# Pooled attention and a bilinear layer on one Trainium2 core: the PSUM tile of the scores, split into five tiles of one bank for the last stage

## The chip, the cores and the metric

The kernel runs on one core of one Trainium2 chip. The metric is the time of one execution on the device in microseconds (us). The engines are named as the profile names them: PE multiplies matrices (PEld is its load of weights), DVE is the vector engine, ACT the scalar engine, POOL the third one for element-wise work, and SP issues the transfers. PE writes its products into PSUM, from where DVE and ACT read them.

## The reference

An attention with pairwise averaged queries feeds a bilinear layer, all in single precision:

```
q_pool = q.reshape(B, H, S // 2, 2, D).mean(axis=3)        # B, H, S, D = 4, 8, 1152, 64
scores = (q_pool @ k.T) / sqrt(D)
attn   = softmax(scores)                                    # with 1e-9 in the divisor
x      = (attn @ v)  as 2304 tokens x 512
out    = ((x @ w_a) * (x @ w_b)) @ w_out                    # 512 -> 1536 -> 512
```

## The kernel before, in words

**Precision.** Most operands are held as a pair of 16-bit numbers, a high and a low part, and a product is the sum of three: high by high, high by low, low by high. So one logical product is a run of several matmuls into one place in PSUM.

**Stages.** The attention goes over 16 pairs of heads in blocks of 128 query rows: scores on PE (`qk`, lines 789 and 791) into `sps`, the running maximum on DVE (`sm_max`, line 821), the exponential and the division on ACT and DVE (lines 828 to 845), a transposing transfer, and the product with v (line 942). The bilinear layer works on nine tiles of 256 tokens. Tiles 0 to 6 go one after the other, between the heads of the attention, each in 12 column blocks: `moe_mm` (line 1023) makes the two products, ACT and DVE multiply them (`moe_a`, `moe_g`), ACT and POOL split the result into its two parts (`moe_gh`, line 1066; `moe_gl`, line 1069), and `moe_o` (line 1089) adds its six matmuls to the output.

**The last stage.** The last two tiles, 7 and 8, are worked jointly, from about 706 us to 831 us of the trace. For each column block f, PE makes seven products (`joint`, line 1263), each six matmuls of 128x256, from sums of weights and sums of tokens. ACT copies the first (`c_copy`, line 1266), DVE adds the others up in seven additions (`c_add`, line 1269) and multiplies the two results (`c_g`, line 1273). Then come `moe_gh`, `moe_gl` and two `moe_o`, one for each tile, of six matmuls of 128x512. In between DVE and POOL prepare the sums of weights for the blocks ahead (`t_sum` line 1203, `t_mix` line 1209, `t_hi` line 1213, `t_lo` line 1217; `bal_w` line 1200).

**Where the products land.** `sps` is one tile of 2560 columns, five banks of 512. In the attention it holds the scores of one block. In the last stage it holds the seven products, which go round four of the banks by `place(f, n)` and use the second half of each, and in the fifth bank one half of the output of tile 7. The other output halves are in `xps` (tile 7) and in `ab0` and `ab1` (tile 8).

```
ab = [PT(f"ab{j}", [128, 2, TOK]) for j in range(2)]
xps = PT("xps", [128, 512])
sps = PT("sps", [128, 2560])
def place(f, n):
    return (len(TURN) * f + TURN.index(n)) % 4
def wide(f, n):
    return sps[:, 512 * place(f, n) + TOK:512 * place(f, n) + 2 * TOK]
```

**What sets the order.** The kernel is described as 3009 tasks, each with the names that it reads and writes (`P0` to `P3` for the four places). A table written out by hand, `ORDERS`, gives the order of the tasks on each of PE, DVE, ACT, POOL and SP. Small products that fill gaps on PE (`idle`, line 651, and `warm`, line 655) are tasks of this table too. The waits themselves are not in the table: the tile framework derives them from which instruction touches which tile.

Of the kernel before, what the change touches and what calls it, by code (L numbers as in the profile page):

```python
# [7 lines left out]
F32 = mybir.dt.float32  # L8
# [32 lines left out]
TOK = 256  # L41
# [56 lines left out]
    ),  # L98
    (
# [240 lines left out]
def kernel(  # L340
# [66 lines left out]
    def PT(name, shape):  # L407
        return ps.tile(shape, F32, name=name)

    sps = PT("sps", [128, 2560])  # L410
    ab = [PT(f"ab{j}", [128, 2, TOK]) for j in range(2)]
    xps = PT("xps", [128, 512])
    sums = xps[:, 510:512]
# [660 lines left out]
    def out_bank(t, u):  # L1074
        if t not in sums_in:
            return acc[u]
        at = sums_in[t][u]
# [447 lines left out]
```

## Time and profile before

| what | value |
|---|---|
| time, median of 3 runs | 837.97 us (835.53 to 839.47) |
| the profiled execution: its time | 840.58 us |
| the profiled execution: its span, first to last instruction | 838.8 us |
| PE busy | 772.4 us, 92% |
| DVE busy | 710.1 us, 85% |
| ACT busy | 574.7 us, 69% |
| POOL busy | 209.6 us, 25% |
| mean granted clock of PE | 0.985 |

The profiled execution is 2.6 us above the median and 1.8 us longer than its own span. Busy PE is modelled: a matmul counts as busy until its result has left, so a run of matmuls that stands alone counts as longer than the same run between others. The idle time before an instruction is put down to the instruction that released it. The rows on which the prediction rests stand further down.

### The profile page before, as it was taken

The page shows a single profiled execution, that of the slowest core. Times are in us where ns is not written, and L with a number is a line of the kernel's source. Part 1 is how long each engine was busy: PE and PEld are TensorE (multiplying, and loading weights), DVE is VectorE, ACT ScalarE, POOL GpSimd, SP SyncE. Part 2 cuts the span into 40 slices and gives each one's busy share as a digit, 9 for nine tenths or more (in the row PEclk, how much of TensorE's full clock was granted, in tenths as well). Part 3 has the DMA queues.
Part 4 walks back from the last instruction along what each step waited for, and adds up shares of the span by engine and source line. Part 5 has one row for each costly group of instructions (what it writes and reads, how often), then busy time and mean ns, then how long its engine had stood idle before and what let it go on. Part 6 is the DMA issues. An engine that isn't in the chain of part 4 may idle for free. (4 is left out here: it accounts for less than half of the span.)

```text
span 838.8 us, 21778 instructions
## 1 busy us (share of the span) xinstructions
PE 772.4 (92%) x8976; PEld 574.6 (69%) x8976; DVE 710.1 (85%) x1411; ACT 574.7 (69%) x960; POOL 209.6 (25%) x269
## 2 busy tenths in 40 slices
PE   9899899999999999999999989999999998677775
PEld 7686687756777667875886578758866884454553
DVE  5988899999889999888899998999899868666572
ACT  6999898898777877677778877777788643212221
POOL 1445141123102321104011401051013251233411
PEclk9999699999999999999999999999999999999998
DMA  8647699999999998778999987998799610000001
GB/s 326 209 131 249 159 259 260 222 206 209 213 185 197 186 198 202 156 170 159 184 198 214 165 214 154 165 186 163 154 196 170 139 31 0 26 1 1 1 0 52
DMA packets 316436, 132.36 MB, mean 158 GB/s; under 512 B 300848, under 2 KB 302896, under 8 KB 316336
## 3 DMA queue, kind: packets, MB, share of 16 engines
q1 hardware_dynamic: 316336, 130.96, 74.5%
q8 instruction: 70, 1.15, 0.6%
q14 instruction: 30, 0.25, 0.1%
HBM read 50.72 MB, written 4.72 MB: 66 GB/s over the span
## 5 line engine op out<-in xcount | busy, mean ns | idle before, releaser
L1023 PE MATMUL ab<-xt,wab 128*128 128x256 f16 x2016 | 229.6, 273 | 0.9 <-DVE st L832 0.5
L1023 PEld LDWEIGHTS <-wab 128*128 128x128 f16 x2016 | 194.7, 99 | 27.1 <-issue 1.8
L828 ACT ACTIVATE s<-s,st 128x1152 f32<-128x1152 f32 x144 | 179.7, 1248 | 34.7 <-DVE s L821 34.5
L845 DVE SCALAR_TENSOR_TENSOR p<-s,st,p 128x1152 f16<-128x1152 f32 x128 | 183.9, 1443 | 11.3 <-ACT p L841 10.1
L841 ACT ACTIVATE p<-s,st 128x1152 f16<-128x1152 f32 x128 | 158.9, 1248 | 39.3 <-issue 12.1
L1069 POOL TENSOR_TENSOR gl<-g,gh 128x256 f16<-128x256 f32 x96 | 75.4, 792 | 332.4 <-ACT gh L1066 254.9
L1089 PE MATMUL ab<-wo,gh 128*128 128x512 f16 x384 | 114.9, 380 | 0.2
L942 PE MATMUL xps<-pt,vs 128*64 128x128 f16 (+1 forms) x3888 | 108.5, 215 | 1.7 <-DVE ksc L477 0.7
L942 PEld LDWEIGHTS <-vs 128*64 128x64 f16 x3888 | 100.7, 110 | 12.9 <-issue 10.2
L821 DVE TENSOR_SCALAR_CACHE_REDUCE s<-sps 128x1152 f32<-128x1152 f32 x72 | 96.4, 1349 | 10.3 <-PE sps L789 8.1
L821 DVE TENSOR_SCALAR_CACHE_REDUCE s<-sps,ksc 128x1152 f32<-128x1152 f32 x72 | 100.7, 1410 | 2.7 <-PE sps L791 1.9
L789 PE MATMUL sps<-k,q 64*128 64x512 f32 (+2 forms) x480 | 89.8, 506 | 3.9 <-DVE s L821 3.6
L1066 ACT ACTIVATE gh<-g 128x256 f16<-128x256 f32 x108 | 42.9, 407 | 61.3 <-DVE g L1273 24.7
L789 PEld LDWEIGHTS sps<-k,q 64*128 64x128 f32 (+1 forms) x480 | 59.4, 178 | 34.6 <-issue 20.7
L1089 PE MATMUL ab<-wo,gl 128*128 128x512 f16 x192 | 72.8, 379 | 1.9 <-POOL gl L1069 1.1
L1089 PEld LDWEIGHTS <-gh 128*128 128x128 f16 x432 | 39.7, 99 | 42.4 <-issue 5.1
L791 PE MATMUL sps<-k,q 64*128 64x512 f16 (+2 forms) x720 | 65.6, 324 | 3.3 <-DVE s L821 3.1
L791 PEld LDWEIGHTS <-q 64*128 64x128 f16 (+1 forms) x720 | 40.2, 96 | 30.6 <-issue 10.1
L1058 ACT ACTIVATE g<-ab 128x256 f32<-128x256 f32 x84 | 30.8, 373 | 32.9 <-PE ab L1023 32.6
L1061 DVE SCALAR_TENSOR_TENSOR g<-ab,cc,g 128x256 f32<-128x256 f32 x84 | 39.6, 478 | 16.2 <-ACT g L1058 15.8
L1203 POOL TENSOR_TENSOR s<-wab 128x512 f32<-128x512 f16 x24 | 30.3, 1272 | 65.9 <-DVE s L1209 19.1
L1266 ACT ACTIVATE q<-sps 128x256 f32<-128x256 f32 x12 | 4.6, 383 | 58.5 <-PE sps L1263 43.6
(195 smaller groups left out, 1030.6 us busy)
## 6 DMA issues: line engine op xcount, KB each, us to landing
k<-in_k_dram SPq DMA_DIRECT2D x18, 576.0 KB, 5.2
vraw<-in_v_dram SPq DMA_DIRECT2D x17, 576.0 KB, 4.4
raw<-in_w_ab_dram SPq DMA_DIRECT2D x18, 512.0 KB, 4.4
qraw<-in_q_dram SPq DMA_DIRECT2D x12, 576.0 KB, 4.7
raw<-in_w_out_dram SPq DMA_DIRECT2D x8, 512.0 KB, 4.8
out_dram<-o SPq DMA_DIRECT2D x16, 256.0 KB, 2.6
xt<-in_w_ab_dram SPq DMA_DIRECT2D x6, 512.0 KB, 4.6
pt<-p SPq DMA_TRANSPOSE x128, 5.4
```

The costliest lines, as they stand in the source:

```text
L789: return nc.tensor.matmul(out, q, k, start=True, stop=True)
L791: return nc.tensor.matmul(out, q[:, hq], k[:, hk], start=(hq, hk) == (0, 0), stop=(hq, hk) == (1, 0))
L821: nc.vector.tensor_scalar(out=s_t[sbuf(i)], in0=sps[:, at:at + S], scalar1=-1.0 / 16.0 if u is None else ksc[:, u, 4:5], scalar2=None, op0 ...
L828: nc.scalar.activation(out=s, in_=s, func=AF.Exp, scale=-1.0, bias=t[:, 0:1], accum_out=t[:, 1:2])
L841: nc.scalar.activation(out=p_t[pbuf(i)][:, 0], in_=s_t[sbuf(i)], func=AF.Copy, scale=st_t[i % NST][:, 3:4])
L845: nc.vector.scalar_tensor_tensor(out=p[:, 1], in0=s, scalar=st_t[i % NST][:, 3:4], in1=p[:, 0], op0=ALU.mult, op1=ALU.subtract)
L942: nc.tensor.matmul(xps[half(e), at:at + w], vs[:, c, e, hv], pt[t][:, hp, c, c0:c0 + w], start=(c == 0 and n == 0), stop=(c == NCH - 1 and ...
L1023: nc.tensor.matmul(dst if t < 8 else dst.rearrange("p (b n) -> p b n", b=B), wab[:, f, 1 - m, a, c], moe_x(t, b, c), start=(n == 0), stop= ...
L1061: nc.vector.scalar_tensor_tensor(out=g_t[:, f], in0=ab[j][:, 0], scalar=cc[:, t, f:f + 1], in1=g_t[:, f], op0=ALU.mult, op1=ALU.mult)
L1066: nc.scalar.activation(out=gh_t[j], in_=g_t[:, f], func=AF.Copy)
L1069: (nc.vector if dve else nc.gpsimd).tensor_tensor(out=gl_t[j], in0=g_t[:, f], in1=gh_t[j], op=ALU.subtract)
L1089: nc.tensor.matmul(out_bank(t, u), g[:, us], wo[:, f, a], start=(first and n == 0), stop=(last and n == 2))
```

## The change

After the last scores have been read, the tile `sps` is given back and its five banks are taken again as five tiles of one bank each (`bank(0)` to `bank(4)`). The seven products go to the first half of `bank(0)` to `bank(3)`, in the same turn, and the output half of tile 7 to `bank(4)`. To be able to give the tile back, `sps` has a pool of its own, which is made after `ab` and `xps`. All five lists of `ORDERS` are new. They hold the same 3009 tasks: none is added, none is left out, and what each computes and waits for by name is the same. Lines after the change are ten further down in this part of the file (1263 becomes 1273, 1269 becomes 1279).

```diff
 ORDERS = (
     (
-        2, 72, 56, 66, 12, 48, 61, 3, 4, 5, 91, 92, 6, 7, 52, 65, 8, 49, 18, 105, 117, 103, 109, 107, 9, 74, 64, 111,
...
+        60, 54, 70, 2, 3, 4, 5, 28, 6, 91, 92, 7, 23, 8, 22, 77, 10, 74, 105, 103, 117, 109, 107, 11, 172, 111, 9,
...
-    sps = PT("sps", [128, 2560])
     ab = [PT(f"ab{j}", [128, 2, TOK]) for j in range(2)]
     xps = PT("xps", [128, 512])
+    scores_pool = tc.tile_pool(name="scores", bufs=1, space=bass.MemoryType.PSUM)
+    sps = scores_pool.__enter__().tile([128, 2560], F32, name="sps")
+    bank_t = []
+
+    def bank(j):
+
+        if not bank_t:
+            scores_pool.__exit__(None, None, None)
+            pool = ctx.enter_context(tc.tile_pool(name="banks", bufs=1, space=bass.MemoryType.PSUM))
+            bank_t.extend(pool.tile([128, 512], F32, name=f"bank{n}") for n in range(5))
+        return bank_t[j]
...
         at = sums_in[t][u]
-        return xps if at is None else sps[:, at:at + 512]
+        return xps if at is None else bank(at // 512)
...
     def wide(f, n):
-        return sps[:, 512 * place(f, n) + TOK:512 * place(f, n) + 2 * TOK]
+        return bank(place(f, n))[:, 0:TOK]
```

PE in the last stage, column block f = 4, before: the products in their order, each shown by the row with which it begins (its five further matmuls and the loads of weights are left out). `sps_122` is the tile, `p1_87` holds the sums of weights of this block, `raw2`, `raw3`, `xr` and `xt1` the tokens, and a wait names the engine on whose count of finished instructions the row waits.

```order
L1263 MATMUL sps_122<-raw3_100,p1_87 128x256 [waits DVE_49]
...
L1263 MATMUL sps_122<-raw2_99,p1_87 128x256
...
L1263 MATMUL sps_122<-xt1_64,wab_61 128x256 [waits Activation_49]
...
L1263 MATMUL sps_122<-raw2_99,p1_87 128x256 [waits DVE_49]
...
L1263 MATMUL sps_122<-xr_65,p1_87 128x256 [waits DVE_49]
...
L1263 MATMUL sps_122<-raw3_100,wab_61 128x256
...
L1089 MATMUL sps_122<-wo_62,gh0_93 128x512 [waits DVE_49]
```

The same block after the change:

```order
L1273 MATMUL bank3_10157<-raw2_99,p1_87 128x256 [waits DVE_49]
...
L1273 MATMUL bank1_10155<-raw2_99,p1_87 128x256
...
L1273 MATMUL bank0_10154<-xt1_64,wab_61 128x256 [waits Activation_49]
...
L1273 MATMUL bank2_10156<-raw3_100,p1_87 128x256 [waits DVE_49]
...
L1099 MATMUL bank4_10158<-wo_62,gh0_93 128x512
...
L1273 MATMUL bank2_10156<-raw3_100,wab_61 128x256 [waits DVE_49]
...
L1273 MATMUL bank1_10155<-xr_65,p1_87 128x256
```

Each product now names the bank that it writes; the product with `xr` and the output product into `bank4` begin without a wait for DVE, and two output products (the one shown, and one into `ab0` and `ab1`) stand between the products of the block.

DVE in the last stage, the additions of the same block, before:

```order
L1269 SCALAR_TENSOR_TENSOR q0_78<-sps_122,q0_78 128x256 [waits PE_49,Activation_49]
L1269 SCALAR_TENSOR_TENSOR x32_66<-sps_122,q0_78 128x256 [waits DVE_49,PE_49]
L1200 TENSOR_SCALAR wab_61<-wab_61,bal_121 128x1024
L1269 SCALAR_TENSOR_TENSOR q1_79<-sps_122,q0_78 128x256 [waits PE_49]
L1269 SCALAR_TENSOR_TENSOR q1_79<-sps_122,x32_66 128x256 [waits DVE_49]
...
L1269 SCALAR_TENSOR_TENSOR q0_78<-sps_122,q0_78 128x256 [waits PE_49]
L1269 SCALAR_TENSOR_TENSOR q1_79<-sps_122,q1_79 128x256
L1269 SCALAR_TENSOR_TENSOR x32_66<-sps_122,x32_66 128x256
```

And after:

```order
L1279 SCALAR_TENSOR_TENSOR x32_66<-bank2_10156,q0_78 128x256 [waits DVE_49,PE_49]
L1279 SCALAR_TENSOR_TENSOR q1_79<-bank3_10157,q0_78 128x256
L1279 SCALAR_TENSOR_TENSOR q1_79<-bank2_10156,q1_79 128x256 [waits DVE_49,PE_49]
L1279 SCALAR_TENSOR_TENSOR q1_79<-bank3_10157,x32_66 128x256
L1279 SCALAR_TENSOR_TENSOR q0_78<-bank0_10154,q0_78 128x256
L1279 SCALAR_TENSOR_TENSOR x32_66<-bank1_10155,x32_66 128x256 [waits DVE_49,PE_49]
```

The preparation that stood among the additions (line 1200, and four subtractions where the dots are) has gone to other places; the additions of this block follow one another in another order.

PE at the very start of the program, before (`xps<-one` are the filling products, `sps` the first scores, `ab<-g,s` transposes):

```order
L651 MATMUL xps<-one 128x256
L655 MATMUL xps<-one 128x96 x6
L651 MATMUL xps<-one 128x256 x3
L789 MATMUL sps<-k_74,q_78 128x512
```

And after:

```order
L665 MATMUL xps<-one 128x96 x3
L661 MATMUL xps<-one 128x256 x4
L665 MATMUL xps<-one 128x96
L661 MATMUL xps<-one 128x256
L799 MATMUL sps<-k_74,q_78 128x512
```

The filling products are the same 78 in all, dealt out anew over the whole program; some that stood in the attention now stand in front of the last stage.

## Rows read from the trace of the kernel before

**Rows 1.** The page, section 4: the chain that ended last, by engine and line.

```profile
PE 26%; DVE 8%; issue 2%; ACT 1%; DMA 0%; SPq 0%; DVEq 0%; ACTq 0%
PE ab L1023 7%; PE sps L1263 6%; PE ab L1089 5%; PE xps L942 3%; PE sps L791 2%; DVE q L1269 2%; DVE x L1269 1%; DVE p L845 1%; PE sps L1089 1%; ACT q L1266 0%; PE xps L1089 0%; DVE s L821 0%; DVE g L1273 0%; DVE pt L1217 0%; DVE s L1209 0%
```

**Rows 2.** Busy time of each engine in five stretches; the first line names the columns.

```profile
core 0: us, PE busy (x) PEld busy (x) DVE busy (x) ACT busy (x) POOL busy (x), PEclk, DMA share, GB/s
0.00:105.00 105.00, 94.10 (x730) 74.30 (x730) 87.05 (x194) 89.47 (x171) 40.46 (x79) 0.90 0.66 215
105.00:650.00 545.00, 528.92 (x7018) 395.98 (x7014) 500.16 (x936) 431.06 (x667) 114.97 (x135) 1.00 0.99 192
650.00:706.00 56.00, 54.47 (x599) 42.01 (x594) 44.18 (x95) 28.05 (x58) 19.56 (x17) 1.00 0.31 64
706.00:831.00 125.00, 94.90 (x645) 62.33 (x643) 77.93 (x187) 25.41 (x67) 34.59 (x38) 1.00 0.01 5
831.00:839.00 8.00, 0.00 (x0) 0.00 (x0) 0.75 (x1) 0.69 (x1) 0.00 (x0) 0.67 0.48 132
```

**Rows 3.** Waits of PE from 706 to 831 us: total, times, longest.

```profile
PE sps L1263 <- DVE q L1269: 15.4, 23, 0.9
PE sps L1263 <- DVE x L1269: 7.5, 11, 1.5
PE sps L1263 <- ACT q L1266: 3.2, 7, 0.5
PE sps L1089 <- DVE q L1269: 2.2, 3, 0.8
PE sps L1089 <- DVE x L1269: 1.0, 2, 0.5
PE sps L1089 <- ACT q L1266: 0.5, 1, 0.5
```

**Rows 4.** Waits of DVE in the same stretch.

```profile
DVE q L1269 <- PE sps L1263: 25.4, 27, 3.4
DVE x L1269 <- PE sps L1263: 9.3, 10, 1.2
DVE q L1269 <- PE sps L1089: 5.8, 5, 1.6
```

**Rows 5.** Timeline within block 4: start, duration, instruction, idle time before it and releaser.

```profile
747.37 0.81 PE L1263 MATMUL sps<-xt,wab 128*128 128x256 f16 x6 [0.47 <-ACT q L1266]
748.29 0.42 DVE L1269 SCALAR_TENSOR_TENSOR q<-sps,q 128x256 f32<-128x256 f32 x1 [0.57 <-PE sps L1263]
748.77 0.82 PE L1263 MATMUL sps<-raw,p 128*128 128x256 f16 x6 [0.58 <-DVE q L1269]
749.62 0.43 DVE L1269 SCALAR_TENSOR_TENSOR x<-sps,q 128x256 f32<-128x256 f32 x1 [0.91 <-PE sps L1263]
...
750.10 0.82 PE L1263 MATMUL sps<-xr,p 128*128 128x256 f16 x6 [0.52 <-DVE x L1269]
750.75 0.82 PE L1263 MATMUL sps<-raw,wab 128*128 128x256 f16 x6
751.61 0.43 DVE L1269 SCALAR_TENSOR_TENSOR q<-sps,q 128x256 f32<-128x256 f32 x1 [1.17 <-PE sps L1263]
...
752.42 0.59 PE L1089 MATMUL sps<-wo,gh 128*128 128x512 f16 x2 [0.85 <-DVE q L1269]
```

**Rows 6.** Stretch 706 to 831 us: line 1263 alone, then line 1089 (PE, PEld, clock).

```profile
706.00:831.00 125.00, 61.89 (x489) 47.17 (x487) 1.00 0.01 5
...
706.00:831.00 125.00, 36.95 (x156) 15.16 (x156) 1.00 0.01 5
```

**Rows 7.** Timeline of PE: products without a wait between them.

```profile
767.18 2.12 PE L1263 MATMUL sps<-raw,p 128*128 128x256 f16 x18 [0.40 <-ACT q L1266]
...
828.12 0.59 PE L1089 MATMUL sps<-wo,gh 128*128 128x512 f16 x2
...
829.42 0.59 PE L1089 MATMUL ab<-wo,gh 128*128 128x512 f16 x2
```

**Rows 8.** Busy time by engine, columns as in the second group, in a stretch of the attention.

```profile
88.00:104.00 16.00, 12.67 (x97) 10.20 (x98) 12.84 (x31) 12.47 (x24) 1.49 (x4) 0.57 0.65 148
```

316 rows, old and new, of the table ORDERS are left out of this document.

## The prediction, on record before the change was run

> **What bounds the kernel now.** I read the busy time by stretch first, then the waits of the stretch that stands out, then its timeline. The chain that ended last shows PE ahead of all others, but it names `sps` of line 1263 and the additions of line 1269 side by side [rows 1], and it shows a quarter of the span only, so the stretches decide. From 105 to 650 us PE is busy 528.9 of 545 us, that is 97%, with DVE at 92%; from 650 to 706 us again 97% [rows 2]. There PE is the bound. From 706 to 831 us, the joint work on the last two tiles, PE is busy 94.9 of 125 us, DVE 77.9, POOL 34.6, ACT 25.4, the transfers next to nothing, and the clock stands at full speed [rows 2]. No engine is full there: something makes them take turns.
>
> The waits say what. PE's waits in this stretch add up to 15.4 + 7.5 + 3.2 + 2.2 + 1.0 + 0.5 = 29.8 us, and every one of them ends with a read of `sps` by DVE or ACT [rows 3]. That is all of PE's idle time (125 - 94.9 = 30.1). At the same time DVE waits 25.4 + 9.3 + 5.8 = 40.5 us for PE to write `sps` [rows 4]. Each waits for the other. The timeline shows the pattern in block 4: a product of six matmuls takes 0.82 us, an addition starts 0.03 to 0.1 us after it, and the next product starts 0.05 us after that addition has ended, and so on in turn [rows 5]. Four products and the step to the output take from 747.37 to 752.42, 5.05 us [rows 5].
>
> The products go round four banks, so a product should have to wait only for the reader of the product four places back. In the built kernel it does not: of the products into `sps` in this stage that wait for a count of DVE or ACT instructions, I followed the count to the instruction that it names, and in 54 of 58 cases it reads another bank than the product writes, as a rule the bank of the product just made. The framework keeps the books for the whole tile. The additions suffer the same way: many wait for a later product than the one that they read.
>
> **The change part by part.** *The split.* With five tiles the books are kept by bank. The same count on the changed kernel gives 56 cases out of 56 in which the read waited for is of the bank that is written, and none of another. So the taking of turns goes, and what is late next is either PE itself or an honest wait: product n+4 for the reader of product n.
>
> What PE needs at least: 489 matmuls of 128x256 and 156 of 128x512 lie in the stretch [rows 6]. Back to back, 18 of the first kind take 2.12 us, which with 0.27 us for the last is 1.85 / 17 = 0.109 us each; six of the second kind go from 828.12 to 829.42, 0.217 us each [rows 7]. 489 x 0.109 + 156 x 0.217 = 53.3 + 33.8 = 87.1 us. The busy time of 94.9 us is larger since each lone product also counts the 0.16 us in which its result leaves. So 125 - 87.1 = 37.9 us is the most that the split can give: 29.8 of waits and 8.1 of such ends.
>
> What stays idle: PE needs 87.1 / 12 = 7.3 us for a block, DVE 77.9 / 12 = 6.5 us, so DVE has 0.8 us of room in each block, not much. The low end is the 3% at which PE idles from 105 to 650 us, with DVE nearly as loaded there [rows 2]: 87.1 / 0.97 is 2.7 us of idle time. The high end is half of today's 37.9, 19 us: the chain through one block stays (copy on ACT, seven additions, two multiplications), the five small buffers of the additions are shared by all blocks, and the copy of the next block must wait for the multiplication that reads its buffer. Today's row prices such a step at some 0.5 us, in the wait for ACT [rows 5], and the new order of DVE puts preparation of later blocks in that place in ten of eleven blocks. PE has up to four products (2.6 us) and one or two output products (1.3 us each) in hand while DVE does such a piece. I take 7 us, nearer to the row of 3% since the loads are like those there, with some more for the first block, where PE waits for the sums of tokens, and the last, where nothing is left to overlap. The stretch then lasts 87.1 + 7 = 94 us, and the gain is 125 - 94 = 31 us, between 19 and 35.
>
> *Giving the tile back.* The first write to a new tile waits until all scores have been read. The table already put the products behind that point, the waiting instruction is on PE, and the last scores are read before the tile 6 products, of which 54 us of busy PE lie in between [rows 2]. This costs nothing here. The end behind the last matmul, 8 us of output steps and stores [rows 2], is the same work in the same order: nothing.
>
> *First half of the bank in place of the second, and other banks for `ab`, `xps` and `sps`.* Same shapes, same banks apart; the rows of 128x256 writes are all 0.27 us, whichever of the four places. I set nothing.
>
> *The new order outside the last stage.* All five lists are dealt anew, DMA issues on SP included, with the same tasks. From 105 to 650 us PE has 16 us of idle time in all [rows 2]; a better order can win a part of it, a worse one can add about as much. In the first 105 us PE stands at a mean clock of 0.90, and between 88 and 104 us at 0.57 with 12.7 us busy [rows 8]: at full speed that work would need some 5 us less, and a second stretch like it would cost as much. I set nothing for all this, with 8 us to either side, as there is no row that speaks for a sign.
>
> A rule of the notes speaks against the split. Rows first: the kernel before goes round four banks, and PE still waits 29.8 us for the reads [rows 3]. The Trainium skill (Perfetto Trace Analysis, section "Optimizing Tensor Performance", on matmuls) says that independent groups of matmuls should rotate through different banks so that the evacuation of one overlaps the next group's matmuls. By that rule the overlap would be there already and the split would give nothing; the trace does not agree, as rotating the banks alone did not bring the overlap.
>
> **Sum.** 840.6 us is the profiled execution. Less 31 gives 809.6 us. It stood 2.6 us above the median of the runs, so against the median I forecast 838.0 - 31 = **807 us**.
>
> **The rivals.** *The chain of one block takes over.* If the copy, the additions and the weights prepared just in time keep half of the idle time, the stretch takes 87.1 + 19 = 106 us and the kernel 838.0 - 19 = 819 us. For it: DVE needs nine tenths of PE's time per block. Against it: the additions that today wait 40.5 us for PE [rows 4] are late because PE is, and PE is late because they are; both ends of that loop go.
>
> *The split does not do what it says.* The readers of a bank are late in fact, not by the books; then the waits [rows 3] stay under new names, and the time is 838 us, give or take the new order. Against it: in the timeline PE starts 0.05 us after a read of another bank [rows 5], three free places notwithstanding.
>
> *Slower than before: the clock of the first stage.* The filling products stand elsewhere now, and some have left the attention for the place in front of the last stage. PE ran at 0.57 from 88 to 104 us when its work came in small pieces [rows 8]. If the new places leave it at the lower of its two levels, 1.2 of 2.4 GHz, for a longer time, every microsecond of work there takes two. This eats the gain of 31 us once 31 us of work at full speed runs at half, a stretch of 62 us; for all of the first 105 us, with 94.1 x 0.90 = 85 us of work at full speed, it would be 170 - 94 = 76 us more, 883 us. Against it: nine fillers in place of ten stand before the first scores, as many as before in all, and DVE and ACT set much of the pace there (87 and 89 of 105 us), so PE has some room.
>
> **How the numbers follow.** Forecast, 807 us: 0.82. Chain of a block, 819: 0.11. No effect, 838: 0.03. Slower by the clock or by a bad new order: 0.04. For the range I put the bounds of the parts together: the stretch from 4 us better (2.7 in place of 7 us idle) to 12 us worse, the rest 8 us to either side, not both at their ends: 807 - 9 = 798 and 807 + 14 = 821, which takes in the rival of the chain. Chances: faster by over 0.5% (4.2 us, about what a measurement of this kernel can tell from no change) 0.82 + 0.11 + 0.01 = 0.94, within 0.5% 0.03 (no effect), slower 0.03; of the last case's 0.04 I leave 0.01 to an order that eats only a part of the gain.
>
> **What would show it.** In the profile after: the joint stage lasts some 94 us in place of 125; PE busy there is 93% or more; waits of PE for DVE and ACT on the banks fall from 29.8 us to under 7 in all; waits of DVE for PE fall from 40 us to around 15; most products stand in runs of several without a gap. The stretch from 105 us to the joint stage keeps its length within 8 us. The forecast is wrong if PE's waits in the joint stage stay above 15 us, or if the granted clock in the first 105 us is well below 0.90.

## The result, and the profile after

The changed kernel takes 804.62 us (median of 4 runs, 803.08 to 807.17), the kernel before 838.6 us beside it. The ratio is 0.960, with a 95% interval of 0.957 to 0.964. The profiled execution takes 803.89 us, 36.7 us less than the 840.58 us of before. In a second, later series the changed kernel took 810.76 us (6 runs, 803.1 to 813.83), at a ratio of 0.967 (0.963 to 0.970). The ten runs together have a median of 807.3 us. What differs between the two series is told with the last experiments.

Where the 36.7 us come from is read with one mark in either kernel: the first product of the joint work, which adds `xt` times `wab` to one of the four places. The rows give count, shortest, median and longest matmul in ns, and the first and the last start. First before, then after:

```profile
L1263 PE MATMUL sps<-xt,wab x144: 269/272/283, 689.7 to 821.2; 128*128 128x256 f16 x144
```

```profile
L1273 PE MATMUL bank<-xt,wab x144: 272/273/273, 688.8 to 786.5; 128*128 128x256 f16 x144
```

Before, the joint work lasts from 689.75 to the last matmul at 830.88, 141.1 us. After, it lasts from 688.84 to 793.96, 105.1 us. That is 36.0 us less. All that comes ahead of it gained 0.9 us in this execution, and the output behind it takes 8 us as before. So the whole gain lies in the joint work.

The busy time by stretch shows the same. The columns are those of [rows 2]; the first row is the attention at its start, the second the middle of the kernel, the third is the end of the tile 6 products with the first joint ones, the fourth the joint stage.

```profile
0.00:105.00 105.00, 90.35 (x746) 72.25 (x747) 88.04 (x195) 89.86 (x172) 44.51 (x83) 0.97 0.70 222
105.00:650.00 545.00, 526.39 (x7016) 394.85 (x7016) 498.74 (x935) 431.91 (x663) 109.15 (x132) 1.00 1.00 191
...
688.00:702.00 14.00, 12.85 (x73) 6.74 (x71) 12.30 (x28) 6.48 (x15) 3.95 (x3) 1.00 0.01 1
702.00:794.00 92.00, 90.99 (x663) 64.66 (x661) 78.12 (x196) 26.00 (x68) 33.68 (x38) 1.00 0.02 7
```

From 702 to 794 us PE is busy 90.99 of 92 us, 99%, where it was 94.9 of 125 [rows 2]. DVE has as much to do as before (78.1 us in place of 77.9), but now 85% of the time.

The waits of PE in this stretch are one row, against the six of [rows 3] with 29.8 us. The second row here is DVE's largest waits for PE, which were 40.5 us in [rows 4]:

```profile
PE bank L1273 <- DVE q L1279: 1.0, 2, 0.5
```

```profile
DVE q L1279 <- PE bank L1273: 6.4, 10, 1.6
DVE o L1105 <- PE xps L1099: 1.6, 1, 1.6
DVE x L1279 <- PE bank L1273: 1.6, 3, 0.8
```

The timeline of PE and DVE in a block shows what became of the turns of [rows 5]. The columns are start, duration, instruction, idle time ahead of it and its releaser.

```profile
737.63 0.82 PE L1273 MATMUL bank<-xr,p 128*128 128x256 f16 x6
737.83 0.42 DVE L1279 SCALAR_TENSOR_TENSOR q<-bank,q 128x256 f32<-128x256 f32 x1 [1.12 <-PE bank L1273]
738.17 0.41 DVE L1279 SCALAR_TENSOR_TENSOR q<-bank,x 128x256 f32<-128x256 f32 x1
...
738.28 0.59 PE L1099 MATMUL bank<-wo,gh 128*128 128x512 f16 x2
...
738.50 0.41 DVE L1279 SCALAR_TENSOR_TENSOR q<-bank,q 128x256 f32<-128x256 f32 x1
...
738.83 0.41 DVE L1279 SCALAR_TENSOR_TENSOR x<-bank,x 128x256 f32<-128x256 f32 x1
...
740.08 1.36 DVE L1227 SCALAR_TENSOR_TENSOR p<-s,p 128x512 f16<-128x512 f32 x3
...
740.24 2.13 PE L1273 MATMUL bank<-raw,p 128*128 128x256 f16 x18
```

PE writes the product with `xr` while DVE reads another bank (737.83), goes on to the output products while four additions run one behind the other, and then makes three products in a row (740.24, 18 matmuls in 2.13 us, the pace of [rows 7]) while DVE prepares weights for a later block. No row of PE here has idle time ahead of it.

The chain that ended last was 26% PE [rows 1]. It is now 14% PE, and DVE's share fell from 8% to 2%. All shares together cover 16% of the span now and 37% before, so the chain is followed back over a shorter stretch, and it says less than the waits do:

```profile
PE 14%; DVE 2%; issue 0%; ACT 0%; DMA 0%; SPq 0%; ACTq 0%; DVEq 0%
```

### The profile page after: what moved, and what is told of

It is laid out like the page before. It is cut to its first block, busy times and chain, and to the rows that moved or that the text cites. A ratio compares the mean times of both kernels' runs of the same rounds, so it can differ in the third digit from the quotient of the medians.

```text
span 802.1 us, 21799 instructions
## 1 busy us (share of the span) xinstructions
PE 758.4 (95%) x8976; PEld 572.1 (71%) x8976; DVE 703.3 (88%) x1411; ACT 576.4 (72%) x960; POOL 207.1 (26%) x269
## 5 line engine op out<-in xcount | busy, mean ns | idle before, releaser
L855 DVE SCALAR_TENSOR_TENSOR p<-s,st,p 128x1152 f16<-128x1152 f32 x128 | 180.9, 1419 | 15.2 <-ACT p L851 13.8
L1079 POOL TENSOR_TENSOR gl<-g,gh 128x256 f16<-128x256 f32 x96 | 77.8, 817 | 311.5 <-ACT gh L1076 257.9
L799 PE MATMUL sps<-k,q 64*128 64x512 f32 (+2 forms) x480 | 88.0, 498 | 4.8 <-DVE s L831 4.6
L993 POOL TENSOR_TENSOR xt<-x,xt 128x256 f16<-128x256 f32 x32 | 22.7, 711 | 84.9 <-ACT xt L989 71.3
L1099 PEld LDWEIGHTS <-gl 128*128 128x128 f16 x216 | 21.1, 98 | 33.0 <-POOL gl L1079 6.0
```

The lines of the kernel that those rows point to most:

```text
L799: return nc.tensor.matmul(out, q, k, start=True, stop=True)
L855: nc.vector.scalar_tensor_tensor(out=p[:, 1], in0=s, scalar=st_t[i % NST][:, 3:4], in1=p[:, 0], op0=ALU.mult, op1=ALU.subtract)
L1079: (nc.vector if dve else nc.gpsimd).tensor_tensor(out=gl_t[j], in0=g_t[:, f], in1=gh_t[j], op=ALU.subtract)
L1099: nc.tensor.matmul(out_bank(t, u), g[:, us], wo[:, f, a], start=(first and n == 0), stop=(last and n == 2))
```

## The experiments

The theory is that the framework keeps its books by tile. With the four places in one tile, a product waits for the reader of the product just made; with a tile for each bank it waits only for the reader of its own bank. Against it stand the new order, the new places in PSUM, and the clock. The ratios compare with the kernel before on the same chip. Its median there is 839.2 us beside the order alone, the split alone, the four banks in one tile and the old order outside the joint stage; 838.5 us beside the two tiles, the first series of the second half and the kernel without filling products; 837.9 us beside the three repeats.

### The order alone, and the split alone

The change has two parts, and each was made without the other. First the new order with the old single tile. Against the kernel before, all five lists differ and nothing else:

```diff
 ORDERS = (
     (
-        2, 72, 56, 66, 12, 48, 61, 3, 4, 5, 91, 92, 6, 7, 52, 65, 8, 49, 18, 105, 117, 103, 109, 107, 9, 74, 64, 111,
...
+        60, 54, 70, 2, 3, 4, 5, 28, 6, 91, 92, 7, 23, 8, 22, 77, 10, 74, 105, 103, 117, 109, 107, 11, 172, 111, 9,
...
```

> The kernel before with the new order lists and nothing else: the scores' tile stays whole. Theory (the books by tile make PE and DVE take turns, and only the split ends that): the joint stage keeps its turns, PE's waits there stay at 25 us or more, the time is 830 to 850 us. Rival (the new order is what gains): the joint stage shrinks to about 95 us, the time is 803 to 812 us.

Measured: 849.8 us, ratio 1.010 (1.004 to 1.016). The order alone makes the kernel about 1% slower. The joint work takes 144.8 us. PE's waits there, from its first product to its last matmul, are much as they were in [rows 3], 31.2 us in all:

```profile
PE sps L1263 <- DVE q L1269: 13.1, 19, 2.0
PE sps L1263 <- DVE x L1269: 8.4, 13, 1.3
PE sps L1263 <- ACT q L1266: 4.5, 9, 1.0
PE sps L1089 <- DVE q L1269: 3.6, 5, 0.8
PE ab L1089 <- DVE gl L1069: 1.1, 2, 0.6
PE sps L1089 <- ACT q L1266: 0.5, 1, 0.5
```

Then the five tiles with the old order. Against the changed kernel, again only the lists differ:

```diff
 ORDERS = (
     (
-        60, 54, 70, 2, 3, 4, 5, 28, 6, 91, 92, 7, 23, 8, 22, 77, 10, 74, 105, 103, 117, 109, 107, 11, 172, 111, 9,
...
+        2, 72, 56, 66, 12, 48, 61, 3, 4, 5, 91, 92, 6, 7, 52, 65, 8, 49, 18, 105, 117, 103, 109, 107, 9, 74, 64, 111,
...
```

> The changed kernel with the order lists of before: five tiles of one bank, old order. Theory: the waits of PE for DVE and ACT in the joint stage fall from 29.8 us to under 10, the stage lasts 91 to 100 us, the time is 804 to 815 us. Rival (the order gains): the stage stays above 115 us, the time is 828 to 840 us.

Measured: 803.21 us, ratio 0.957 (0.955 to 0.959), a little under the range expected. The split alone brings all of the gain. The joint work takes 106.3 us against the 105.1 of the changed kernel, and PE's waits there are 3.1 us in all:

```profile
PE bank L1273 <- DVE q L1279: 1.2, 2, 0.7
PE bank L1273 <- DVE x L1279: 0.8, 1, 0.8
PE ab L1099 <- DVE gl L1079: 0.8, 1, 0.8
PE bank L1273 <- ACT q L1276: 0.3, 1, 0.3
```

So in the joint work the two orders differ by 1.2 us once the books are kept by bank. It may be the preparation of weights, which the old order puts among the additions; no run moves that alone.

### How far the split has to go

The changed kernel does more than split: the tile is given back, the products move to another half of the bank, and all comes from another pool. In the next kernel everything of that stays but the split among the four places of the products:

```diff
-            bank_t.extend(pool.tile([128, 512], F32, name=f"bank{n}") for n in range(5))
+            four = pool.tile([128, 2048], F32, name="four")
+            bank_t.extend(four[:, 512 * n:512 * n + 512] for n in range(4))
+            bank_t.append(pool.tile([128, 512], F32, name="bank4"))
```

> The changed kernel, but the four banks of the seven products are one tile of 2048 columns again and only the output bank has its own; new order, own pool, first halves of the banks as in the change. Theory: the turns come back for the products, only the waits at the output bank stay gone, PE waits 20 us or more in the joint stage, the time is 825 to 845 us. Rival (it is the new pool, the half of the bank or the place in PSUM that gains): 803 to 808 us.

Measured: 839.7 us, ratio 0.999 (0.996 to 1.002). No gain is left in the median time. In the profiled execution, the fastest of the ten with 835.13 us, the joint work takes 134.6 us, and PE waits for readers again, 23.6 us in the three rows of `four`:

```profile
PE four L1275 <- DVE q L1281: 11.1, 18, 1.1
PE four L1275 <- DVE x L1281: 8.0, 12, 1.3
PE four L1275 <- ACT q L1278: 4.5, 9, 1.0
```

The rows of output products that waited for a reader of `sps` (4.1 us with the order alone) are absent here, since the output bank has a tile of its own. That is worth something: the joint work is 6.5 us shorter than in the kernel before (141.1 us). The 144.8 us of the order alone hold a fall of the clock besides (last section). By the start of the same additions in both traces, the kernel with the order alone is 8.1 us later ahead of that fall (755.5 against 747.4 us) and 11.6 us later behind it (766.3 against 754.7 us). So some 3.5 us go there, 0.8 of them in the wait of an output product.

Then two tiles of two banks, places 0 and 1 in one and 2 and 3 in the other:

```diff
-            bank_t.extend(pool.tile([128, 512], F32, name=f"bank{n}") for n in range(5))
+            two = [pool.tile([128, 1024], F32, name=f"two{n}") for n in range(2)]
+            bank_t.extend(two[n // 2][:, 512 * (n % 2):512 * (n % 2) + 512] for n in range(4))
+            bank_t.append(pool.tile([128, 512], F32, name="bank4"))
```

> The changed kernel, but the four banks of the products are two tiles of two banks (places 0 and 1 in one, 2 and 3 in the other); the output bank keeps a tile of its own, the order is that of the changed kernel. Theory (the books are kept by tile, and each reader of a tile holds up the next write to that tile): between the two ends, since neighbours in turn share a tile in half of the cases: PE's waits in the last stage between those of one tile of four (about 25 us) and those of four tiles (1.5 us), I set 8 to 15 us, and the time 811 to 825 us. Rival (any split gives PE something else to do during a read, so the second tile brings the whole gain): 803 to 807 us. Other rival (a pair is as bad as all four): 835 to 840 us.

Measured: 815.67 us, ratio 0.972 (0.966 to 0.978). The joint work takes 111.5 us, 6.4 us more than with four tiles and 23.1 less than with one. PE waits 5.8 us for readers of a pair:

```profile
PE two L1275 <- DVE q L1281: 2.6, 5, 0.8
PE two L1275 <- DVE x L1281: 1.9, 2, 1.5
PE two L1275 <- ACT q L1278: 1.3, 3, 0.5
```

So waits and time go down with each division, as the theory has it; that two tiles would leave 8 to 15 us of waits was too much. In the timeline output products often stand between the products, which PE can make while a pair is read; that this is the reason is not shown. The time of 815.67 us is not the joint work alone: in this execution the joint work began at 698.2 us, 9.4 us later than in the profiled one of the changed kernel, which has the same order up to there. By the start of the same instructions of DVE in both traces, 3.5 us are lost by 110 us, with a mean clock of 0.91 against 0.97 up to there, 3.0 more at 150 us, where DVE waits 3.5 us for a transfer in place of 0.5, and 1.4 at about 310 us, where the clock falls; more on this below.

### The half of the bank

```diff
-        return bank(place(f, n))[:, 0:TOK]
+        return bank(place(f, n))[:, TOK:2 * TOK]
```

> The changed kernel with one thing undone: the seven products go to the second half (columns 256 to 511) of their banks again, as before the change, in place of the first. Theory (the gain is the split among the four banks alone, the half costs and brings nothing): 803 to 808 us, the last stage about 105 us from its first product to its last output matmul, PE's waits on the banks there 1 to 3 us. Rival (the place within the bank takes part in the gain): some us more, with products or additions that last longer than 0.27 and 0.42 us.

Measured: 809.96 us, ratio 0.967 (0.963 to 0.971), some 5 us above the changed kernel's first series and 2 us above the range expected. The joint work is just as long (from 693.6 us to the last matmul, 105.1 us), and the products and PE's waits are the same. What differs lies ahead of it. So the pair was run again on one chip, with the split alone as the third.

> Products in the second half of the banks, beside the unaltered changed kernel on the same chip. In its first runs it took 809.96 us with a last stage just as long as the changed kernel's, and started that stage 5 us later. Theory (the half is worth nothing, the 5 us were the clock in the first 110 us, from run to run): within 3 us of the changed kernel's repeat. Rival (the half costs something): again 4 us or more above it.

> The changed kernel itself, once more, beside the variant with the second half of the banks and the variant with the old order, on one chip. It tells how far a difference of 5 us between two variants is one of the chip and of the run. Theory: 803 to 810 us; what differs from run to run is the granted clock in the first 110 us, not the last stage, which keeps 105 us.

Measured: 808.92 us with the second half (ratio 0.966, 0.963 to 0.969), 810.76 us for the changed kernel itself (0.967, 0.963 to 0.970), just above its expected range. The half of the bank costs nothing that can be told: the joint work takes 105.1 us in the profiled execution of each of the four series. The 5 us between the first series belong to the runs. The clock of the first 110 us, which was expected to be the reason, is a small part of them: by the start of the same instructions 0.8 of 4.8 us are lost by then. The next section takes such a difference apart.

### The order outside the joint stage

> The five tiles with the old order of the tasks, on the same chip as the repeat of the changed kernel. Theory (the new order brings nothing beside the split): within 0.5% of that repeat, in either direction; the last stage 106 us to the changed kernel's 105. Rival (the new order is worth something): over 4 us above it.

Measured: the split with the old order takes 805.19 us (ratio 0.961, 0.959 to 0.964) beside the 810.76 us of the changed kernel, 0.7% less, where 0.5% either way was expected. Over both series it has a median of 803.6 us (9 runs, 802.7 to 806.6) against 807.3 us (10 runs, 803.1 to 813.8). So the old order with the five tiles is no slower than the changed kernel, and by these medians some 0.5% faster, at the edge of what can be told. It is the best version found.

Where the changed kernel loses time in some executions is seen in the trace of its repeat. There PE waits 2.3 us for POOL at 304 us. Busy time by engine and, third from the end, the granted clock, in pieces of 2 us:

```profile
304.00:306.00 2.00, 0.12 (x1) 0.00 (x0) 2.00 (x3) 0.06 (x1) 2.00 (x2) 1.00 1.12 206
306.00:308.00 2.00, 1.57 (x4) 0.40 (x4) 1.12 (x2) 0.21 (x1) 1.73 (x2) 0.67 1.16 217
308.00:310.00 2.00, 2.00 (x57) 1.89 (x57) 0.49 (x3) 1.45 (x3) 0.00 (x0) 0.50 1.14 210
310.00:312.00 2.00, 2.00 (x12) 1.20 (x13) 1.31 (x4) 0.53 (x2) 0.00 (x0) 0.98 0.73 134
```

PE does next to nothing from 304 to 306 us, then the clock falls to the lower of its two levels (0.50 of full speed, 1.2 of 2.4 GHz) until about 310 us, and the work there runs at half speed. The same happens at 184 us, behind a wait of 2.1 us for DVE. Between 110 and 650 us the longest waits of PE in this kernel are, with total, times and longest:

```profile
PE sps L799 <- DVE s L831: 3.9, 3, 2.1
PE ab L1099 <- POOL gl L1079: 3.5, 3, 2.3
```

With the old order and the five tiles the same two waits are at most 1.0 and 0.6 us long in the first series (1.2 and 0.6 in the second), those for `s` at the other line of scores 1.3 us, and the clock stands at 1.00 all the way from 110 to 650 us:

```profile
PE sps L801 <- DVE s L831: 4.0, 5, 1.3
PE sps L799 <- DVE s L831: 3.4, 6, 1.0
PE xps L665 <- ACT x L965: 1.8, 3, 0.8
PE ab L1099 <- POOL gl L1079: 1.1, 3, 0.6
```

The joint work starts 7.3 us later in this execution than in the first one of the changed kernel (696.1 against 688.8 us). Both run the same order, so the start of the same instruction of DVE in either trace tells where they were lost. By 125 us the repeat is 1.5 us late, nearly all of it since 88 us; from 88 to 104 us the mean clock is 0.68 against 0.79 (0.94 against 0.97 in the first 110 us). The largest step, 2.6 us, comes at 146 us, where the granted clock is 1.00: DVE waits for the last piece of `w_out`. The rows show the issue of its transfer and the instruction that waits for it, in the first execution and in the repeat:

```profile
141.66 0.53 SPq L619 DMA_DIRECT2D xt<-in_w_out_dram  x1
146.23 0.69 DVE L623 TENSOR_REDUCE wmx<-xt 128x1 f32<-128x512 f32 x1 [0.49 <-DMA xt<-in_w_out_dram]
```

```profile
144.02 0.53 SPq L619 DMA_DIRECT2D xt<-in_w_out_dram  x1
150.33 0.69 DVE L623 TENSOR_REDUCE wmx<-xt 128x1 f32<-128x512 f32 x1 [3.05 <-DMA xt<-in_w_out_dram]
```

In the other kernels with the new order this wait is 0.3 to 3.5 us long. The old order issues this transfer at 138 to 140 us, and there the wait is at most 0.25 us. Around the two falls of the clock the repeat loses 0.6 and 1.4 us, at about 442 us another 0.8. The depth of a fall alone would say more: a mean clock of 0.83 over 10 us is 1.7 us, but from 180 to 190 us DVE is busy 9.97 of 10 us, which may be why a slower PE costs less there.

```profile
180.00:190.00 10.00, 7.90 (x80) 5.76 (x80) 9.97 (x16) 7.72 (x14) 3.43 (x4) 0.83 1.21 191
300.00:310.00 10.00, 7.69 (x83) 4.93 (x82) 7.48 (x12) 5.56 (x8) 5.02 (x4) 0.83 1.14 213
0.00:110.00 110.00, 96.23 (x771) 77.33 (x773) 90.32 (x205) 93.82 (x177) 46.42 (x84) 0.94 0.70 219
```

In its first execution the changed kernel has the same two waits (2.1 and 2.3 us), and the clock stayed at 1.00 behind both. So a wait of this length sometimes ends with a fall of the clock and sometimes not; what decides it, the runs do not show. The kernel with the second half of the banks had both falls in its first series and the later one in its second, the order alone had both, the one with two tiles the later one. Four banks in one tile and the kernel without filling products had none, with waits of up to 2.3 and 2.4 us, and with the old order there were none. So the spread of the times, 803 to 814 us for the changed kernel and 802.7 to 806.6 for the old order with five tiles, has several sources: the first 110 us, the transfer of `w_out` and the falls. In the profiled executions with the new order the joint work starts between 688.8 and 698.2 us (eight of them), with the old order between 687.6 and 690.3 us (three). Nor does the old order keep the times together by itself: the kernel before took 837.3 to 845.2 us in 13 runs on one chip.

An attempt to have the changed kernel's last stage behind the old order was less clear. In each list the tasks up to the last stage stand as they did before, and those of the last stage follow one another as in the changed kernel, in the places that the old list has for such tasks:

```diff
 ORDERS = (
     (
-        60, 54, 70, 2, 3, 4, 5, 28, 6, 91, 92, 7, 23, 8, 22, 77, 10, 74, 105, 103, 117, 109, 107, 11, 172, 111, 9,
...
+        2, 72, 56, 66, 12, 48, 61, 3, 4, 5, 91, 92, 6, 7, 52, 65, 8, 49, 18, 105, 117, 103, 109, 107, 9, 74, 64, 111,
...
```

> The changed kernel; the tasks of the last stage (tile 6 of the bilinear layer and all that follows) stand in the new order among themselves, all others as in the lists of before. Theory (the order outside the last stage is worth nothing clear): 802 to 809 us, and the joint stage lasts 91 to 94 us as after the change. Rival (a part of the gain comes from the new order in the attention): 810 us or more with the same short joint stage.

Measured: 809.45 us, ratio 0.965 (0.961 to 0.968), just above the range expected. The joint work takes 105.3 us, but the two orders don't fit where they meet: PE is busy 34.04 of 41 us from 650 to 691 us, with one wait of 3.3 us for a transfer and one of 2.9 us for DVE, where the kernel before had 97% in about the same place [rows 2].

```profile
650.00:691.00 41.00, 34.04 (x433) 30.11 (x431) 24.81 (x51) 15.70 (x33) 14.35 (x12) 1.00 0.41 74
```

The 7 us of that seam hide what the order ahead of it is worth, so nothing follows from this kernel but that the joint work is 105 us long behind either order. The clock stays at 1.00 through the seam, behind waits longer than those of the repeat.

### The filling products

One rival had the clock of the first stage hang on where the filling products stand. This kernel leaves all 78 of them out.

```diff
-        nc.tensor.matmul(xps[:, 0:256], one.broadcast_to([128, 128]), one.broadcast_to([128, 256]), start=True, stop=True)
+        pass
...
-        nc.tensor.matmul(xps[:, 384:480], one.broadcast_to([128, 128]), one.broadcast_to([128, 96]), start=True, stop=True)
+        pass
```

> The changed kernel without its filling products (the 78 small matmuls of the helpers idle and warm are left out; nothing reads what they write, so no part of the output is missing). It tests the rival of the prediction that the filling products' places decide over the clock in the first stage. If they hold the clock up: in the first 105 us the mean granted clock falls from 0.97 to between 0.7 and 0.9, and the time grows by 5 to 25 us (85 us of work at full speed at a mean clock of 0.8 is 21 us more, of which some is hidden since PE idles there for 15 us). If they don't: the clock keeps 0.95 or more and the time is within 3 us of 804.6.

Measured: 806.48 us, ratio 0.961 (0.958 to 0.965). In the first 105 us PE does 80.4 us of work in place of 90.4, and the clock is 0.95 against 0.97:

```profile
0.00:105.00 105.00, 80.35 (x640) 61.15 (x642) 85.69 (x192) 87.20 (x168) 41.74 (x81) 0.95 0.69 219
```

The repeated changed kernel, with its fillers, had 0.94 in the first 110 us, so the difference is within what executions differ by. The fillers hardly carry the clock here, and their places can't have cost what the rival asked for.

## Why the prediction was right, point by point

**What bounds the kernel.** Right: PE and DVE took turns because of the books of one tile. One tile for the four places gives 839.7 us, a tile for each 804.6 and 810.8 us, with all else the same.

**The size of the gain in the joint stage.** The mechanism was right, the term for what stays idle was too large, and with it the gain too small. 37.9 us was the most that could go, 7 us were set for remaining idle time (2.7 to 19), which left 31. The joint work became 36.0 us shorter, so 37.9 - 36.0 = 1.9 us stayed, below even the low end. PE's waits from 688.8 us on, 1.0 us on a bank (shown above) and 1.1 us on `ab`, are of that size:

```profile
PE ab L1099 <- DVE gl L1079: 1.1, 2, 0.6
```

The prices of the matmuls hold too: from 702 to 794 us there are 492 of the smaller and 171 of the larger kind, 90.7 us at 0.109 and 0.217 us each, in 92 us. The low end was taken from the stretch from 105 to 650 us, where PE idles 3%, since DVE's load is about the same there. What that row does not have is the choice PE has in the joint stage: up to four products and two output products stand ready while DVE does other work. The prediction named these, and then put the term on the side of the row. That this choice is what made the difference is argued; no run takes it away.

**The chain of one block** (819 us) did not take over. Both ends of the loop went, as argued: DVE's waits for PE on the banks fell from 40.5 us to 6.4 + 1.6 = 8.0 us, lower than the 15 set, and the wait for the copy is absent.

**Giving the tile back, and the other places in PSUM:** nothing, as set. The second half of the bank gives 808.92 us beside 810.76 us.

**The new order outside the last stage** was set at nothing, 8 us to either side. The bounds held for the changed kernel; there is a sign, though. Alone it costs about 1% (849.8 us). In its profiled execution 5.5 us of that lie ahead of the joint work (start at 695.3 in place of 689.75 us), with a wait of 3.2 us for `w_out` and both falls of the clock; in the joint work most of the 3.6 us more goes with the fall at 756 us (the last section). With the split it cost 5.6 us in the second series and nothing that can be told in the first; with two tiles the joint work started 8.5 us later than before. The order of before has no wait of PE above 1.3 us between 110 and 650 us; what the new order made of that, and of the transfer of `w_out`, was not to be read from the trace of before.

**The split does nothing** (838 us) is excluded by the split alone, 803.21 us. **The clock of the first stage** did not fall: 0.97 in the first 105 us in place of 0.90 [rows 2], and 0.79 from 88 to 104 us in place of the 0.57 of [rows 8]:

```profile
88.00:104.00 16.00, 12.89 (x119) 10.17 (x120) 13.10 (x31) 12.58 (x26) 4.48 (x6) 0.79 0.80 181
```

This is one execution. The same order gave 0.68 from 88 to 104 us in the repeat and 0.58 with two tiles, so the better clock does not belong to the order.

**The rule against the split.** The Trainium skill (Perfetto Trace Analysis, section "Optimizing Tensor Performance") asks to rotate independent groups of matmuls through different banks, so that the evacuation of one overlaps the next. The kernel with four places in one tile does rotate, by the same table as the changed one, and PE waits 23.6 us there; with a tile for each bank it waits 1.0 us. So in this kernel the overlap that the rule promises came only once the books were split as well.

**What would show it.** A joint stage of 94 us in place of 125: since 36.0 us went, it comes to 89. PE busy 93% or more: 99%. Waits on the banks under 7 us: 1.0. The way to the joint stage within 8 us: 0.9 us less in the first series, 6.4 us more in the second. The time of 807 us was within 3 us of the first series, 4 us of the second and 0.3 us of the median of all ten runs. That it is so close is in part luck: a gain that was 5 us too small met later starts of the joint work in several executions, which take some of it back.

## What to carry to other kernels

When two engines wait for each other on one buffer, look which part of it each wait is really for. If products rotate through parts of a tile and still wait for the reader of the last one, the dependencies may be kept for the whole tile: make each part a tile of its own, and test it by splitting only that. A new order of the rest is to be judged apart from it and over several runs. Where two executions of one order differ, compare the start of the same instruction in both traces, before a cause is named.

## What the runs showed that was not expected

A wait of PE of 2.1 to 2.3 us in the middle of the kernel can be followed by 3 to 4 us at the lower level of the clock; in other executions of the same kernel it is not, and waits of 2.9 and 3.3 us in the kernel with the old order outside were followed by none. In the repeated changed kernel the two falls go with 2.0 of the 7.3 us by which its joint work starts later. A wait of DVE for a transfer, which differs from execution to execution with one and the same order, goes with more, 2.6 us. With the new order alone a fall came in the joint stage too. PE waited 2.01 us there for an addition, the longest of the 19 such waits, and the clock fell right behind it, to stay low until about 763 us (0.50 from 760 to 762 us, 0.59 from 762 to 764):

```profile
754.00:756.00 2.00, 0.27 (x2) 0.00 (x0) 2.00 (x4) 0.35 (x2) 1.29 (x1) 1.00 0.00 0
756.00:758.00 2.00, 1.72 (x11) 1.33 (x11) 0.23 (x1) 0.00 (x0) 0.00 (x0) 0.70 0.00 0
758.00:760.00 2.00, 1.16 (x5) 0.46 (x4) 0.76 (x2) 0.00 (x0) 0.00 (x0) 0.50 0.00 0
```

The kernel before kept full speed through its joint stage with a fourth of PE's time idle, in waits of at most 1.5 us [rows 2, 3].
